# A state-space layer and a gated feed-forward in one kernel: the second x tile and the second up row change queues, and the first tile runs ahead alone

## The chip, the core and the metric

The kernel runs on one core of a Trainium2 chip. A core has a matrix engine (TensorE, in the profile PE, its weight loads PEld), VectorE (DVE), ScalarE (ACT), GpSimd (POOL) and SyncE (SP). SP, ACT and POOL issue transfers (DMAs); ACT's and SP's go through hardware queues, POOL's through a software queue. The metric is the device time of one execution in microseconds (us), and the shown time is the median over several executions.

## The reference

For x of 2048 tokens and 512 features, with xn the layer norm of x:

```python
xn = _layernorm(x, axis=-1)
return x + _A_ref(xn, ...) + _B_ref(xn, w_gate, w_up, w_down)

# _A_ref: a diagonal complex state-space model of 512 states
Bu = jnp.einsum("bld,pd->blp", x + 0j, B_bar)
h = Lam_bar[None, :] * h + Bu[:, t, :]          # for each t of 2048
y = 2.0 * jnp.einsum("blp,dp->bld", hseq, Cmat).real + x * Dskip

# _B_ref: a gated feed-forward with 1376 hidden features
return (silu(x @ w_gate) * (x @ w_up)) @ w_down
```

Inputs, weights and output are bfloat16. The products run in bfloat16 with sums in float32.

## The kernel before, in words

The 2048 tokens are cut into 16 tiles of 128, and these into four chunks of 512. For each chunk the kernel does the projection into the states (`bproj_tile`, L382), the scan over time (VectorE, L429, with rotations around it), the gate and up products (`gu_mm`, L459), and the two products that give the output (`out_ffn` L623, `out_ssm` L633). The 1376 hidden features are ten blocks of 128 and a last part of 96, which has a function of its own (`gateup_last`, L548): sixteen small matmuls into two PSUM banks, two activations and two copies on ACT, and a product on VectorE that is put into the list `products` and issued later, together with the transpose of the result.

TensorE's order is written out by hand. VectorE's work for scans, tables and norms stands in a backlog with costs, and `pump(us)` issues as much of it as the given matmul time covers; `multiply(keep)` issues waiting products until `keep` are left. Every engine works off its own instructions in the order in which the code issues them.

Chunk 0 starts differently from the others, since nothing is loaded yet. Its first three tiles have the tokens as the fixed operand of the matmul and the weights as the moving one, so that the work can follow the weights row by row: a "row" (`load_row`, L121) is 128 of the 512 input features of a weight for hidden features 0 to 1023, 128 x 1024 values or 256 KB. There are four up rows (`wu01`, indices 0 to 3), four gate rows (`wg01`), and one transfer each for the remaining features (`w_end`). All of these are issued by SP in one line, behind tile 0 of x; tile 1 of x is issued by ACT. A VectorE memset of two elements of tile 1 stands ahead of that ACT transfer, which therefore waits for it. POOL loads three small parameter vectors.

For tiles 0 and 1 the normalization does not wait for the statistics. `sum_dve` (L228) sums each token's features on VectorE; `raw_mm` (L240) transposes the raw tile on TensorE, in four blocks `k` of 128 features; `cT_mean` (L244) subtracts the mean in the same PSUM bank with a further matmul; `raw_copy` (L248) copies each block to SBUF (`xcT`), the even ones on ACT, the odd ones on VectorE. These blocks are the fixed operands of `row_mm(which, k)` (L747, matmuls at L506), which multiplies row `k` with both tiles and both halves of the features: four matmuls of 512 columns. The factor 1/std is applied when ACT takes the result out of PSUM (`sw_up` L522, `sw_gate` L512).

The order at the head is: sums of both tiles, transposes of tile 0, half of its means and copies, transposes of tile 1, the other means, the other copies, then `row_mm` for up rows 0 to 3, the statistics (`ln_stats` L188) of tiles 0 and 1, gate rows, and tiles 2 and 3. Then follow the rest of chunk 0's features (L813), the projection of chunk 0 (L865), which needs the transposed weight `BT` (`load_bt`, L148), `gateup_last(0)` (L878), and chunk 1's projection.

Of the kernel before, what the change touches and what calls it, by code (L numbers as in the profile page):

```python
# [23 lines left out]
def kernel(  # L24
# [17 lines left out]
    nc = tc.nc  # L42
# [9 lines left out]
    KD = D // 128  # L52
# [25 lines left out]
    def bank(shape=(128, CW), dtype=F32):  # L78
        return psum.tile(list(shape), dtype, name="ps")

    def flat(ap3):
        return ap3.rearrange("p q j -> p (q j)")

    x_v = A_x[0].rearrange("(n p) d -> p n d", p=128)
    out_v = out[0].rearrange("(n p) d -> p n d", p=128)
    wg_v = B_w_gate.rearrange("(k p) f -> p k f", p=128)
    wu_v = B_w_up.rearrange("(k p) f -> p k f", p=128)


    xall = const.tile([128, NT, D], BF16, name="xall")  # L90
# [5 lines left out]
    wu01 = const.tile([128, KD, FE], BF16, name="wu01")  # L96
# [24 lines left out]
    def load_row(q, t, view, k):  # L121
        q.dma_start(out=t[:, k, :], in_=view[:, k, 0:FE])  # L122

    HK = KD // 2
# [1 line left out]
    make_identity(nc, ident[:])  # L126
    minus_mean = const.tile([128, 128], BF16, name="minus_mean")
    nc.sync.dma_start(out=xall[:, 0, :], in_=x_v[:, 0, :])  # L128
    nc.vector.memset(xall[:, 1, 0:2], 0.0)
    nc.scalar.dma_start(out=xall[:, 1, :], in_=x_v[:, 1, :])  # L130
    nc.scalar.preload_act_table_set("silu_and_others")
    for k in range(KD):
        load_row(nc.sync, wu01, wu_v, k)
    for k in range(HK):
        load_row(nc.sync, wg01, wg_v, k)
# [49 lines left out]
    def by_k(ap):  # L185
        return ap.rearrange("p (k d) -> p k d", d=128)
# [36 lines left out]
    sums = const.tile([128, 2], BF16, name="sums")  # L223
# [4 lines left out]
    def sum_dve(i, dst):  # L228
        nc.vector.scalar_tensor_tensor(out=xnT[:, NCH - 1, i, 0:HW], in0=xall[:, i, 0:HW], scalar=1.0,
                                       in1=xall[:, i, HW:D], op0=ALU.mult, op1=ALU.add, accum_out=dst)  # L230
# [3 lines left out]
    raw = [pair[0][1] + pair[1][0], pair[1][1] * 2]  # L234

    def cT_mm(ps, src, k, first, stop):
        nc.tensor.matmul(ps[:, k * 128:(k + 1) * 128], lhsT=src[:, k * 128:(k + 1) * 128], rhs=ident[:], start=first,  # L237
                         stop=stop)

    def raw_mm(i):  # L240
        for k in range(KD):
            cT_mm(raw[i][k], xall[:, i, :], k, all(p is not raw[i][k] for p in raw[i][:k]), False)

    def cT_mean(i, *ks):  # L244
        nc.tensor.matmul(by_k(raw[i][ks[0]][:])[:, ks[0]:ks[-1] + 1:HK], lhsT=sums[:, i:i + 1].to_broadcast([128, 128]),
                         rhs=minus_mean[:, None, :].to_broadcast([128, len(ks), 128]), start=False, stop=True)

    def raw_copy(i, k):  # L248
        cT_copy(V.tensor_copy if k % 2 else nc.scalar.copy, raw[i][k], i, k, k + 1)

    def cT_copy(copy, ps, i, k0=0, k1=KD):
        copy(out=xcT[:, k0:k1, i * 128:(i + 1) * 128], in_=by_k(ps[:, k0 * 128:k1 * 128]))
# [21 lines left out]
    V = nc.vector  # L274
# [107 lines left out]
    def bproj_tile(c, part, q):  # L382
        if c not in u_tiles:
            u_tiles[c] = ssm.tile([128, 2, NQ, CW], BF16, name="u16", bufs=2)
        ps = bank()
        for k in range(KD):
            nc.tensor.matmul(ps[:] if c else by_k(ps[:]), lhsT=BT[:, part, k, q * 128:(q + 1) * 128],  # L387
                             rhs=xnT[:, c, k, :] if c else xnT0[:, k], start=(k == 0), stop=(k == KD - 1))
        nc.scalar.copy(out=u_tiles[c][:, part, q, :], in_=ps[:])  # L389
# [67 lines left out]
    products = []  # L457
# [10 lines left out]
    def gu_tile(c):  # L468
        if c not in gu_tiles:
            gu_tiles[c] = gut.tile([128, FT, CW], BF16, name="guT")  # L470
        return gu_tiles[c]
# [8 lines left out]
    def gu_rest(c):  # L480
        return gu_more_rest[:] if c == 2 else gu_tile(c)[:, FT - 1, 0:RT * 128]
# [21 lines left out]
    def sw_mm(ps, groups, gi, i, k0=0, k1=KD):  # L503
        a, b = fgroups[gi]
        for k in range(k0, k1):
            nc.tensor.matmul(ps[:, 0:(b - a) * 128], lhsT=tokens(i, k), rhs=groups[gi][:, k, 0:(b - a) * 128],  # L506
                             start=(k == 0), stop=(k == KD - 1))
# [35 lines left out]
    def g0_dma(a, b):  # L543
        nc.sync.dma_start_transpose(out=runs(gu_tiles[0][:, a:b, :]), in_=g0[:, a:b].rearrange("p f i d -> p (f i d)"))
# [3 lines left out]
    def gateup_last(c):  # L548
        gl = g_last[c % 2][:] if c else g0[:, FT - 1, 0:RT]
        u = up_p.tile([128, RT, 128], BF16, name="ul", bufs=2)  # L550
        for h in range(0, TPC, 2):
            ps = bank()[:, 0:4 * FR].rearrange("p (i w f) -> p i w f", i=2, w=2)
            for i in range(2):
                for k in range(KD):
                    nc.tensor.matmul(ps[:, i],  # L555
                                     lhsT=xnT[:, c, k, (h + i) * 128:(h + i + 1) * 128] if c else xnT0[:, k, h + i, :],
                                     rhs=w_end[:, k, :, FL - FE:FL - FE + FR], start=(k == 0), stop=(k == KD - 1))
            two = slice(h * RB, (h + 2) * RB)
            src = ps.rearrange("p i w (j f) -> p w j i f", f=RB)
            nc.scalar.activation(out=gl[:, :, two].rearrange("p j (i f) -> p j i f", f=RB), in_=src[:, 0], func=ACT.Silu)  # L560
            nc.scalar.copy(out=u[:, :, two].rearrange("p j (i f) -> p j i f", f=RB), in_=src[:, 1])

        def product():
            V.tensor_tensor(out=gl, in0=gl, in1=u[:], op=ALU.mult)
            if c:
                nc.sync.dma_start_transpose(out=gu_rest(c).rearrange("p (n t) -> p n t", t=128),
                                            in_=gl.rearrange("p i d -> p (i d)"))
            else:
                a = fgroups[1][1]
                n = (FT - 1 - a) * TPC + RT  # L570
                nc.sync.dma_start_transpose(
                    out=flat(gu_tile(0)[:, a:FT, :])[:, 0:n * 128].rearrange("p (n t) -> p n t", t=128),
                    in_=g0[:, a:FT].rearrange("p f i d -> p (f i d)")[:, 0:n * 128])
        products.append(product)
# [93 lines left out]
    def step():  # L668
        for item in backlog[0:AHEAD + 1]:
            if item[2] is not None:  # L670
                item[2]()
                item[2] = None
        cost, op, _, _ = backlog.pop(0)
        op()
        owed[0] -= cost

    def pump(us):

        owed[0] += us
        while backlog and owed[0] >= backlog[0][0] * 0.5:  # L680
            step()
        if not backlog:
            owed[0] = 0.0

    def multiply(keep):

        while len(products) > keep:
            products.pop(0)()
            owed[0] -= 0.65

    def need(tag):

        while any(item[3] == tag for item in backlog):
            step()


    GU = 8 * 0.2163
# [29 lines left out]
    dummy(warm, 4, CW)  # L727
    dummy(warm, 5, 128)
    nc.vector.tensor_scalar(out=minus_mean[:], in0=ident[:], scalar1=-1.0 / D, scalar2=None, op0=ALU.mult)
    for i in range(2):  # L730
        sum_dve(i, sums[:, i:i + 1])
    raw_mm(0)
    for k in range(HK):
        cT_mean(0, k)
        raw_copy(0, k)
    raw_mm(1)
    for k in range(HK, KD):
        cT_mean(0, k)
    for k in range(HK):
        cT_mean(1, k, k + HK)  # L740
        raw_copy(1, k)
    for k in range(HK, KD):
        raw_copy(0, k)
    for k in range(HK, KD):
        raw_copy(1, k)

    def row_mm(which, k):  # L747
        for i in range(2):
            for gi in range(2):
                sw_mm(pair[which][i][gi], (U, G)[which], gi, i, k, k + 1)  # L750

    for k in range(KD):
        row_mm(0, k)
    for i in range(2):
        ln_stats(i)
        ln_rstd(i, i + 1)
# [3 lines left out]
    for n in range(2):  # L760
        norm_dve(n)
    row_mm(1, 0)
    pp = prm_transpose()
    ln_stats(2)
# [6 lines left out]
    for k in range(1, SW):  # L771
        row_mm(1, k)
# [48 lines left out]
    def bproj_chunk(c):  # L821
        need(f"ln{c}")
        for part in range(2):
            for q in range(NQ):
                bproj_tile(c, part, q)
                pump(BP)
                multiply(0 if q else 1)
# [34 lines left out]
        queue(f"ssm{c}", fwd + back)  # L862

    need("ln0")
    for part in range(2):  # L865
        for q in range(NQ):
            bproj_tile(0, part, q)
            pump(BP)
            multiply(0 if q else 1)
# [5 lines left out]
    queue("cf", c_ops())  # L875
    need("ln1")
    g0_dma(0, fgroups[1][1])
    gateup_last(0)  # L878
    pump(GU / 2)
    bproj_chunk(1)  # L880
    load_down()
    for part, src in enumerate((A_C_re, A_C_im)):
# [62 lines left out]
```

## Time and profile before

| what | us |
|---|---|
| median of 3 runs | 177.39 (177.05 to 178.04) |
| the profiled execution's own time | 178.12 |
| its span, first to last instruction | 176.0 |
| TensorE busy | 171.0 |
| VectorE busy | 157.4 |
| ScalarE busy | 102.3 |
| GpSimd busy | 27.1 |

How to read it: times in the views are microseconds from the span's start. A row of the timeline has start, duration, engine, line, operation, output and input tiles, shapes and a count; behind it in brackets the idle time of that engine just ahead and what ended it. In a list of waits, a row has the waiting engine and line, what it waited for, the total, the number of times and the longest. In the table by stretches, a row has the stretch, its length, busy time and number of instructions of PE, PEld, DVE, ACT and POOL, the clock granted to TensorE, the busy share of the DMA engines and GB/s. The chain that ended last gives start, duration and place of each piece. Matmuls overlap, so that several of them in a row take less than the sum of their durations.

### The profile page before, as it was taken

How to read it: one execution, taken by the hardware profiler on the slowest of the kernel's cores; microseconds unless marked ns; L12 is line 12 of the kernel's file. 1: busy time of each engine (PE TensorE's matmuls, PEld its weight loads, DVE VectorE, ACT ScalarE, POOL GpSimd, SP SyncE). 2: the span in 40 equal slices, each digit the busy share in tenths (PEclk: the TensorE clock that was granted, in tenths of full speed). 3: DMA queues.
4: the chain of work that ended last, by engine and by line, in shares of the span. 5: the costliest groups of instructions: out<-in, count | busy, mean ns of one | idle time of the engine just before them, and what ended most of it. 6: DMA issues, size and time to landing. Idle time of an engine off the chain costs nothing.

```text
span 176.0 us, 2435 instructions
## 1 busy us (share of the span) xinstructions
PE 171.0 (97%) x878; PEld 82.0 (47%) x894; DVE 157.4 (89%) x260; ACT 102.3 (58%) x188; POOL 27.1 (15%) x36
## 2 busy tenths in 40 slices
PE   8899999999999999999999999999999999999993
PEld 5444445564444464444444444446444444444542
DVE  3767999999999999999999999999999999589642
ACT  3179589794996689976044362014666652983100
POOL 5234110022000000000302500014100000530700
PEclk9999999999999999999999999999999999999999
DMA  5998969999999300220005830006310000597741
GB/s 152 370 342 80 194 110 181 303 202 293 169 207 274 115 4 0 50 61 0 2 4 111 94 34 0 0 4 68 53 22 0 0 4 0 70 164 124 93 89 60
DMA packets 34027, 18.05 MB, mean 103 GB/s; under 512 B 24512, under 2 KB 32832, under 8 KB 33888
## 3 DMA queue, kind: packets, MB, share of 16 engines
q1 hardware_dynamic: 30272, 14.39, 35.0%
q0 software_dynamic: 3456, 3.28, 14.6%
q10 hardware_dynamic: 288, 0.23, 0.4%
q8 instruction: 7, 0.11, 0.3%
q14 instruction: 4, 0.03, 0.1%
HBM read 8.33 MB, written 5.24 MB: 77 GB/s over the span
## 4 chain that ended last, share of the span: by engine, by line
PE 94%; DMA 3%; issue 1%; SPq 0%; ACT 0%; DVE 0%; ACTq 0%
PE ps L462 29%; PE ps L630 20%; PE ps L643 16%; PE ps L387 16%; PE ps L506 7%; PE ps L555 3%; DMA wu<-in_B_w_up_dram 3%; PE ps L805 2%; PE ps L620 2%; ACT u L489 0%; SPq L122 0%; SPq L128 0%; DVE xall L646 0%; PE ps L237 0%; PE ps L278 0%
## 5 line engine op out<-in xcount | busy, mean ns | idle before, releaser
L429 DVE TENSOR_TENSOR_SCAN g<-r_t,car,u 128x512 bf16<-128x512 f32 x24 | 28.8, 1263 | 0.0
L643 PE MATMUL ps<-CF,wt 128*128 128x512 bf16 (+2 forms) x133 | 28.2, 366 | 0.2
L387 PE MATMUL ps<-xnT,BT 128*128 128x512 bf16 x125 | 28.1, 379 | 0.2
L630 PE MATMUL ps<-wd_sb,guT 128*128 128x512 bf16 (+2 forms) x129 | 26.5, 362 | 0.1
L462 PE MATMUL ps<-xnT,wu 128*128 128x512 bf16 x94 | 24.5, 379 | 0.2
L462 PE MATMUL ps<-xnT,wg 128*128 128x512 bf16 x93 | 24.3, 379 | 0.1
L389 ACT CAST u<-ps 128x512 bf16<-128x512 f32 x32 | 17.8, 591 | 5.0 <-PE ps L387 4.1
L489 ACT CAST u<-ps 128x512 bf16<-128x512 f32 x30 | 17.8, 592 | 4.8 <-PE ps L462 4.8
L643 PEld LDWEIGHTS <-wt 128*128 128x128 bf16 x136 | 12.9, 98 | 15.0 <-DVE xall L600 0.4
L387 PEld LDWEIGHTS <-BT 128*128 128x128 bf16 x128 | 12.5, 98 | 14.9 <-DMA BT<-in_A_B_re_dram 0.3
L630 PEld LDWEIGHTS <-guT 128*128 128x128 bf16 x130 | 12.4, 98 | 13.8
L199 POOL TENSOR_TENSOR rstd<-ve,neg_half 128x1 f32<-128x1 f32 (+1 forms) x7 | 7.0, 1001 | 73.0 <-DVE ve L198 72.6
L652 ACT CAST res<-ps 128x512 bf16<-128x512 f32 x12 | 6.9, 582 | 18.5 <-PE ps L643 18.5
L592 ACT ACTIVATE xr<-xall,nb,rstd 128x512 bf16<-128x512 bf16 x16 | 11.8, 804 | 8.7 <-DVE xall L600 5.0
L653 POOL DMA_DIRECT2D out_dram<-res x12 | 10.5, 1043 | 35.6 <-ACT res L652 30.0
L462 PEld LDWEIGHTS <-wu 128*128 128x128 bf16 x96 | 9.4, 98 | 11.3
L488 ACT ACTIVATE guT<-ps 128x512 bf16<-128x512 f32 x20 | 12.1, 604 | 4.0 <-PE ps L462 3.6
L462 PEld LDWEIGHTS <-wg 128*128 128x128 bf16 x96 | 9.3, 98 | 10.6
L212 ACT ACTIVATE xn<-xall,nb,rstd 128x512 bf16<-128x512 bf16 x8 | 6.3, 816 | 8.8 <-DVE nb L202 8.8
L189 DVE BATCH_NORM_STATS2 stats<-xall 128x6 f32<-128x512 bf16 x16 | 10.8, 675 | 0.6 <-DMA xall<-in_A_x_dram 0.6
L462 PE MATMUL ps<-xnT,w_end 128*128 128x512 bf16 x47 | 10.8, 379 | 0.1
L397 DVE TENSOR_TENSOR pm<-g,c 128x2048 bf16<-128x2048 bf16 x8 | 9.8, 1222 | 0.1
(132 smaller groups left out, 235.3 us busy)
## 6 DMA issues: line engine op xcount, KB each, us to landing
out_dram<-in_A_x_dram SPq DMA_DIRECT2D x8, 192.0 KB, 3.2
out_dram<-res POOLq DMA_DIRECT2D x12, 128.0 KB, 3.1
out_dram<-xall POOLq DMA_DIRECT2D x3, 512.0 KB, 6.4
wd_sb<-in_B_w_down_dram SPq DMA_DIRECT2D x1, 1280.0 KB, 7.8
wu<-in_B_w_up_dram SPq DMA_DIRECT2D x4, 256.0 KB, 4.9
wg<-in_B_w_gate_dram SPq DMA_DIRECT2D x4, 256.0 KB, 5.5
xall<-in_A_x_dram SPq DMA_DIRECT2D x1, 1024.0 KB, 7.0
xall<-in_A_x_dram SPq DMA_DIRECT2D x1, 512.0 KB, 6.1
```

What stands on the lines that cost most here:

```text
L189: nc.vector.bn_stats(out=stats[:, n, 0, :], in_=xall[:, n, :])
L387: nc.tensor.matmul(ps[:] if c else by_k(ps[:]), lhsT=BT[:, part, k, q * 128:(q + 1) * 128], rhs=xnT[:, c, k, :] if c else xnT0[:, k], star ...
L389: nc.scalar.copy(out=u_tiles[c][:, part, q, :], in_=ps[:])
L429: V.tensor_tensor_scan(out=g()[:, part, q, :], data0=r_t[:, q:q + 1].to_broadcast([128, CW]), data1=u_tiles[c][:, part, q, :], initial=ini ...
L462: nc.tensor.matmul(ps[:fs, lo:hi], lhsT=wslice(groups, fi, k), rhs=xnT[:, c, k, lo:hi], start=(k == 0), stop=(k == KD - 1))
L488: nc.scalar.activation(out=gu(c, fi, fi + 1)[:fs, 0, :], in_=psg[:fs], func=ACT.Silu)
L489: nc.scalar.copy(out=u_pair[c][:fs, fi % 2, :], in_=psu[:fs])
L506: nc.tensor.matmul(ps[:, 0:(b - a) * 128], lhsT=tokens(i, k), rhs=groups[gi][:, k, 0:(b - a) * 128], start=(k == 0), stop=(k == KD - 1))
L592: nc.scalar.activation(out=box["xr"][:], in_=xall[:, n, :], func=ACT.Identity, scale=rstd[:, n:n + 1], bias=nb[:, n:n + 1])
L630: nc.tensor.matmul(o_tiles[n, b][:, 0:hi - lo], lhsT=gu(c, fi, fi + 1)[:, 0, i * 128:(i + 1) * 128], rhs=wd_sb[:, fi, lo:hi], start=(fi == ...
L643: nc.tensor.matmul(o[:, 0:hi - lo], lhsT=w_tiles[c][:, part, q, i * 128:(i + 1) * 128], rhs=CF[:, part, q, lo:hi], start=False, stop=(part ...
L653: nc.gpsimd.dma_start(out=out_v[:, n, lo:hi], in_=res[:, lo:hi], accum_op=ALU.add)
```

## The change

Up row 1 is issued by ACT where tile 1 of x was, with the small memset now in that row; SP issues tile 1 of x behind up row 0, and then up rows 2 and 3. VectorE sums tile 0 alone at first. TensorE prepares tile 0 completely, then multiplies it with up rows 0 and 1; only then is tile 1 summed, transposed and copied, with all four copies on ACT. Row 2 follows for tile 0, rows 0 to 2 for tile 1, and row 3 for both. Last, the matmuls of `gateup_last(0)` stand ahead of chunk 0's projection, and its product is taken out of the list and put back at its old place, so that VectorE's order stays as it was.

```diff
-    nc.vector.memset(xall[:, 1, 0:2], 0.0)
-    nc.scalar.dma_start(out=xall[:, 1, :], in_=x_v[:, 1, :])
+    nc.vector.memset(wu01[:, 1, 0:2], 0.0)
+    load_row(nc.scalar, wu01, wu_v, 1)
     nc.scalar.preload_act_table_set("silu_and_others")
-    for k in range(KD):
+    load_row(nc.sync, wu01, wu_v, 0)
+    nc.sync.dma_start(out=xall[:, 1, :], in_=x_v[:, 1, :])
+    for k in range(HK, KD):
         load_row(nc.sync, wu01, wu_v, k)
...
-        cT_copy(V.tensor_copy if k % 2 else nc.scalar.copy, raw[i][k], i, k, k + 1)
+        cT_copy(V.tensor_copy if k % 2 and i == 0 else nc.scalar.copy, raw[i][k], i, k, k + 1)
...
-    for i in range(2):
-        sum_dve(i, sums[:, i:i + 1])
+    def row_mm(which, k, tiles=range(2)):
+        for i in tiles:
+            for gi in range(2):
+                sw_mm(pair[which][i][gi], (U, G)[which], gi, i, k, k + 1)
+
+    sum_dve(0, sums[:, 0:1])
     raw_mm(0)
-    for k in range(HK):
+    for k in range(KD):
         cT_mean(0, k)
         raw_copy(0, k)
+    for k in range(HK):
+        row_mm(0, k, (0,))
+    sum_dve(1, sums[:, 1:2])
     raw_mm(1)
-    for k in range(HK, KD):
-        cT_mean(0, k)
     for k in range(HK):
         cT_mean(1, k, k + HK)
+    for k in range(KD):
         raw_copy(1, k)
-    for k in range(HK, KD):
-        raw_copy(0, k)
-    for k in range(HK, KD):
-        raw_copy(1, k)
...
-    for k in range(KD):
-        row_mm(0, k)
+    row_mm(0, HK, (0,))
+    for k in range(HK + 1):
+        row_mm(0, k, (1,))
+    row_mm(0, KD - 1)
...
     need("ln0")
+    gateup_last(0)
+    pump(GU / 2)
+    last0 = products.pop()
     for part in range(2):
...
     g0_dma(0, fgroups[1][1])
-    gateup_last(0)
-    pump(GU / 2)
+    products.append(last0)
     bproj_chunk(1)
```

Here `KD` is 4 and `HK` is 2.

More of the change, by code (lines that the diff above doesn't have):

```diff
@@ L729 @@
     nc.vector.tensor_scalar(out=minus_mean[:], in0=ident[:], scalar1=-1.0 / D, scalar2=None, op0=ALU.mult)
-    for i in range(2):
-        sum_dve(i, sums[:, i:i + 1])
+    def row_mm(which, k, tiles=range(2)):
[3 more added lines that the diff above has]
+    sum_dve(0, sums[:, 0:1])
     raw_mm(0)
-    for k in range(HK):
+    for k in range(KD):
         cT_mean(0, k)
         raw_copy(0, k)
+    for k in range(HK):
+        row_mm(0, k, (0,))
+    sum_dve(1, sums[:, 1:2])
     raw_mm(1)
-    for k in range(HK, KD):
-        cT_mean(0, k)
     for k in range(HK):
         cT_mean(1, k, k + HK)
+    for k in range(KD):
         raw_copy(1, k)
-    for k in range(HK, KD):
-        raw_copy(0, k)
-    for k in range(HK, KD):
-        raw_copy(1, k)
[L747 to L750, printed above, removed]
-    for k in range(KD):
-        row_mm(0, k)
+    row_mm(0, HK, (0,))
+    for k in range(HK + 1):
+        row_mm(0, k, (1,))
+    row_mm(0, KD - 1)
     for i in range(2):
```

## The prediction

> **What bounds the kernel now.** I read the engines' totals first, then the waits of TensorE, then the chain that ended last, and then the first ten microseconds in order of time.
>
> ```profile
> span 176.0 us, 2435 instructions
> PE 171.0 (97%) x878; PEld 82.0 (47%) x894; DVE 157.4 (89%) x260; ACT 102.3 (58%) x188; POOL 27.1 (15%) x36
> ```
> ```profile
> PE ps L703 <- PEq L929: 0.8, 1, 0.8
> PE ps L506 <- DMA wu<-in_B_w_up_dram: 0.6, 1, 0.6
> ```
>
> TensorE is busy for 97% of the span, and its list of waits has only two entries: the program's start, and one wait of 0.6 us for an up row. The chain tells the same story.
>
> ```profile
> 1.20 0.41 SPq L122
> 1.61 0.04 issue
> 1.65 4.80 DMA wu<-in_B_w_up_dram
> 6.45 0.04 issue
> 6.49 3.61 PE ps L506 x16
> ...
> 22.47 0.86 PE ps L805 x4
> 23.33 6.91 PE ps L387 x32
> 30.24 1.32 PE ps L555 x16
> ```
>
> It runs from the second of the four up rows (row 1, issued at 1.65, landed at 6.45) into TensorE and never leaves it for more than a moment. So the end of the kernel is the time at which TensorE gets through the up rows, plus work without gaps. Whatever the change does to the moment when the first gate matmul starts (9.08 below) comes out at the end unreduced; everything later has to be shown to stay hidden.
>
> The head in order of time (tile 0 and tile 1 are the first two 128-token tiles of x):
>
> ```profile
> 0.90 0.37 ACTq L130 DMA_DIRECT2D xall<-in_A_x_dram  x1
> 3.07 0.42 DVE L229 SCALAR_TENSOR_TENSOR xnT<-xall 128x256 bf16<-128x256 bf16 x1 [1.53 <-DMA xall<-in_A_x_dram]
> 3.09 0.61 PE L237 MATMUL ps<-ident,xall 128*128 128x128 bf16 x4
> 3.48 0.43 DVE L229 SCALAR_TENSOR_TENSOR xnT<-xall 128x256 bf16<-128x256 bf16 x1
> 3.56 0.39 PE L245 MATMUL ps<-minus_mean,sums 128*128 128x128 bf16 x2
> 3.75 0.63 PE L237 MATMUL ps<-ident,xall 128*128 128x128 bf16 x4
> 3.89 0.27 ACT L252 CAST CF<-ps 128x128 bf16<-128x128 f32 x1 [1.30 <-PE ps L245]
> 4.18 0.85 PE L245 MATMUL ps<-minus_mean,sums 128*128 128x128 bf16 x4
> 4.82 1.07 PE L506 MATMUL ps<-wu,CF 128*128 128x512 bf16 x4
> 4.85 0.60 ACT L252 CAST CF<-ps 128x128 bf16<-128x128 f32 x3 [0.69 <-PE ps L245]
> 5.67 0.68 DVE L189 BATCH_NORM_STATS2 stats<-xall 128x6 f32<-128x512 bf16 x1
> 6.49 2.75 PE L506 MATMUL ps<-wu,CF 128*128 128x512 bf16 x12 [0.60 <-DMA wu<-in_B_w_up_dram]
> 9.08 1.03 PE L506 MATMUL ps<-wg,CF 128*128 128x512 bf16 x4
> 9.55 0.69 DVE L189 BATCH_NORM_STATS2 stats<-xall 128x6 f32<-128x512 bf16 x1 [0.60 <-DMA xall<-in_A_x_dram]
> ```
>
> Four matmuls of row 0 are done by 5.89, TensorE stands until 6.49, and twelve more take it to 9.08: (9.08 - 6.49) / 12 = 0.216 us each. Now the transfers, as busy time of each engine and, last, the DMA engines' share and GB/s:
>
> ```profile
> 2.00:2.50 0.50, 0.50 (x3) 0.20 (x2) 0.00 (x0) 0.50 (x1) 0.50 (x2) 1.00 0.93 285
> 2.50:3.00 0.50, 0.50 (x6) 0.41 (x4) 0.00 (x0) 0.09 (x1) 0.50 (x1) 1.00 1.12 367
> 3.00:3.50 0.50, 0.50 (x6) 0.34 (x4) 0.43 (x3) 0.00 (x0) 0.50 (x2) 1.00 1.11 389
> 3.50:4.00 0.50, 0.50 (x7) 0.44 (x6) 0.42 (x4) 0.11 (x1) 0.04 (x1) 1.00 0.80 111
> 4.00:4.50 0.50, 0.50 (x7) 0.50 (x6) 0.29 (x1) 0.15 (x1) 0.00 (x0) 1.00 1.04 226
> 4.50:5.00 0.50, 0.50 (x4) 0.34 (x3) 0.00 (x0) 0.15 (x1) 0.00 (x0) 1.00 0.95 320
> ```
> ```profile
> L506 PE MATMUL ps<-wu,CF x16: 376/379/427, 4.8 to 8.9; 128*128 128x512 bf16 x16
> DMA to landing us min/median/max: 2.9/4.9/5.2
> ```
>
> Two things are to be seen. The DMA engines are full from about 2.5 us on (shares of 0.93 to 1.12), except for a dip between 3.5 and 4.5 where they are occupied but move little. And row 0 (the 2.9 in the second fence, issued at 1.20) lands at 4.1, just before that dip, while row 1 takes 4.8 us. Summing GB/s times 0.5 us gives 697 kB by 4.5 and 857 kB by 5.0. Tile 0, tile 1, row 0 and row 1 are 128 + 128 + 256 + 256 = 768 KB, or 786 kB, which on average had moved by about 4.8. Row 1 yet landed at 6.45: some of the engines lag behind the mean by more than a microsecond, and a landing needs all of them.
>
> **The change, part by part.**
>
> *Order of transfers.* Row 1 takes tile 1's place on the Activation queue (same place, one issue of 0.37 us), tile 1 goes behind row 0 on SP. SP has five issues ahead of the gate rows in both kernels, so rows 2 and 3 and all that follows are issued at the same places, and the bytes ahead of each are the same. The later transfers that wait on an early one's slot (gate row 2 and x 3 now behind up rows 1 and 0, gate row 3 behind tile 1) have a backlog in front of them; I cost this at nothing, with delays under a microsecond hidden by that backlog.
>
> What lands when? Before, row 1 was the last of 768 KB; now tile 1 is the last of the same 768 KB. With full DMA engines, tile 1 inherits row 1's landing, 6.45. Row 0 shares the engines with row 1 and comes later than 4.1; row 1 comes earlier. Bounds for tile 1's landing T: 4.8 (the mean engine) and 6.45 (the slowest). I take the upper for the sum, because it is the measured landing of the same amount of data, and keep the lower for the range.
>
> In sentences of their own: the Trainium skill, "DMA: Bandwidth & Descriptors", section "Issuing engines are not separate DMA queues", says that transfers from all issuing engines end on the same 16 DMA engines and interleave, and that a second issuing engine saves only issue time. By that rule T stays at 6.45; if the Activation queue were a road of its own, SP's 512 KB up to tile 1 would land as early as row 0 did, at 4.1. The full shares with both queues active (1.12 from 2.5 to 3.0) agree with the rule.
>
> *Order of TensorE.* Before, four matmuls stand before the wait and twelve behind: first gate matmul at T + 0.04 + 12 x 0.216 = T + 2.63 (or 5.89 + 2.59 = 8.48 where T is under 5.85). After, tile 1's preparation stands behind the wait instead. From T: the DVE sum and the step to the mean matmul (3.07 to 3.56) with the 0.04 of the wake-up, 0.53; mean to the copy's start (3.56 to 3.89), 0.33; the copy, 0.27; wake-up, 0.04. That is T + 1.17. The transposes of tile 1 lie beside the sum, the two tile-0 matmuls of row 2 (0.43) lie beside mean and copy. Then ten matmuls are left (rows 0 to 2 of tile 1, row 3 of both): 2.16. The first gate matmul starts at T + 3.33. The four copies are now all on ACT, at 0.20 each (0.60 for three) against 0.43 us of matmuls per row, so they do not hold it up; VectorE saves two copies.
>
> The difference is 3.33 - 2.63 = +0.70 us at T = 6.45. The gap has not gone; a transfer with a longer tail behind it now ends it. At T = 5.5, before would start the gate rows at 8.48 and after at 8.83, +0.35; the two are equal at T = 5.15.
>
> *Queued behind the new wait on VectorE.* Tile 1's sum now stands ahead of the statistics of tile 0, which move from 5.67 to T + 0.55 = 7.0, 1.33 later. VectorE's idle 0.60 before 9.55 takes part of that; the rest, 0.73, goes on to tile 2.
>
> ```profile
> 10.50 0.35 DVE L226 TENSOR_SCALAR CF<-xall,mv 128x512 bf16<-128x512 bf16 x1
> 11.51 0.43 PEld L237 LDWEIGHTS <-CF 128*128 128x128 bf16 x4
> 23.10 6.65 PEld L387 LDWEIGHTS <-BT 128*128 128x128 bf16 x32 [0.26 <-DMA BT<-in_A_B_re_dram]
> 38.15 2.35 DVE L397 TENSOR_TENSOR pm<-u,s 128x2048 bf16<-128x2048 bf16 x2
> ```
>
> Tile 2's centring would end at 10.85 + 0.73 = 11.58, and its transposes come at 11.51 + 0.70 = 12.21: hidden. The rest of VectorE's work is 0.73 later with a TensorE that is 0.70 later.
>
> *Last features of chunk 0 first.* Sixteen matmuls (1.32 us in the chain) move from behind the projection to ahead of it. The number is the same, so this costs nothing by itself. It could gain only a wait for BT; the weight load waited 0.26 us for it, but TensorE itself goes from 22.47 + 0.86 to 23.33 without a gap. Gain nothing; were TensorE 0.5 us earlier or BT 0.7 later, these 1.32 us would cover it. The projection's outputs come 1.32 us later on ACT; their first reader on VectorE starts at 38.15, some 7 us behind the projection's end at 30.24. The product is held back to its old place.
>
> The sum: the profiled execution took 178.12 us (176.0 and 2.1 around it), so 178.8 with the same landings. That execution is 0.73 above the median of 177.39; part of that may be its own 0.6 us wait. Against the median the sum gives 178.1 at T = 6.45 and 177.75 at T = 5.5. I take 178.0, nearer the measured landing.
>
> **The rivals.**
>
> *Tile 1 lands early; faster.* The dip between 3.5 and 4.5 may catch other packets now, with two queues open. If tile 1 landed at 4.8, TensorE would be bound by its own work: tile 0's first copy ends at 4.16, so matmuls from about 4.3, sixteen of them (3.46) and tile 1's preparation (0.43 from 3.75 to 4.18), 8.2 in all. That is 0.88 under 9.08 and 0.28 under 8.48: 176.5 to 177.1. It decides from T under 5.15. For it: the mean engine is there at 4.8. Against it: a landing needs the slowest. Chance 0.15.
>
> *The change does not do what it says.* The landings move about as much as the tail behind them costs (T near 5.2): 177.4. Chance 0.20.
>
> *A slow array.* The weight loads of the 512-column warm-up matmuls show their pace:
>
> ```profile
> 1.16 0.15 PEld L703 LDWEIGHTS <-const-bfloat16-1.0 128*128 128x128 bf16 x1 [0.28 <-issue]
> 1.59 0.15 PEld L703 LDWEIGHTS <-const-bfloat16-1.0 128*128 128x128 bf16 x1 [0.28 <-issue]
> ```
>
> One in 0.43 us, half the rate of the 0.216 later. TensorE now has nothing from about 4.3 until row 0 lands, which by the shared engines may be at 5.7. If that idle kept the array slow for eight more matmuls, 8 x 0.21 = 1.7 us would be added: 179.8. Against it: the 0.6 us without work before did not slow the twelve matmuls behind it. Chance 0.10. The Trainium skill, "TensorE: Matmul & The Clock Gate", section "What's actually happening", says that the clock goes to full rate after a busy window of some 3.4 us and that the windows run freely; by it a thinner first window could postpone full rate by one window.
>
> **How the numbers follow.** My forecast, tile 1 ending the wait late and the kernel 0.3 to 1.0 us slower, has 0.55, with its own range 177.7 to 178.6. The measurement can tell about 0.5%, 0.89 us, from no change: 176.5 to 178.28. The forecast lies mostly inside; its upper end (before's median without a gap, 8.48, against 6.45 + 3.33 = 9.78, which is +1.3) lies outside, and with the slow array gives 0.24 for slower. The early landing must be set against a before with its gap to pass 0.5%: 0.06. Within 0.5%: 0.70. The range reaches from 176.9, inside the early case, to 178.8, the sum on the profiled execution.
>
> **What would show it.** Right: a wait of VectorE's L231 and TensorE's L247 for tile 1, ended by an x transfer landing near 6 us; the first gate matmul near 9.4 to 9.8; the 16 matmuls of the last features directly behind L805's last ones, and no new wait beyond 10 us. Wrong: tile 1 landing by 5, the first gate matmul at 8.5 or before, or TensorE waiting for row 0 and then running at 0.43 us a matmul.

## The result and the profile after

The changed kernel takes 178.39 us (median of 22 executions, 177.86 to 180.01) against 177.64 us (177.05 to 178.43): +0.75 us, ratio 1.0046 with a 95% interval of 1.0033 to 1.0059. That is slower, clear of no change; the interval lies on both sides of the 0.5% that the prediction took as the limit of what can be told from no change. The totals and TensorE's list of waits, from the profile of the changed kernel:

```profile
span 176.4 us, 2434 instructions
PE 171.7 (97%) x878; PEld 82.0 (46%) x894; DVE 157.1 (89%) x258; ACT 103.6 (59%) x190; POOL 27.1 (15%) x36
```
```profile
PE ps L705 <- PEq L931: 0.8, 1, 0.8
PE ps L508 <- ACT CF L254: 0.2, 1, 0.2
```

The wait for an up row, 0.6 us before, is gone from this execution, and yet the span is 0.4 longer. The head in order of time (start, duration, engine and line; the lines are two higher than before):

```profile
3.26 0.43 DVE L231 SCALAR_TENSOR_TENSOR xnT<-xall 128x256 bf16<-128x256 bf16 x1 [1.72 <-DMA xall<-in_A_x_dram]
3.28 0.61 PE L239 MATMUL ps<-ident,xall 128*128 128x128 bf16 x4
4.08 0.48 ACT L254 CAST CF<-ps 128x128 bf16<-128x128 f32 x2 [1.49 <-PE ps L247]
4.60 1.86 PE L508 MATMUL ps<-wu,CF 128*128 128x512 bf16 x4 [0.24 <-ACT CF L254]
4.91 0.42 DVE L231 SCALAR_TENSOR_TENSOR xnT<-xall 128x256 bf16<-128x256 bf16 x1 [0.22 <-DMA xall<-in_A_x_dram]
5.41 0.15 PEld L508 LDWEIGHTS <-CF 128*128 128x128 bf16 x1 [0.28 <-issue]
5.83 0.15 PEld L239 LDWEIGHTS <-xall 128*128 128x128 bf16 x1 [0.28 <-issue]
6.26 0.61 PE L239 MATMUL ps<-ident,xall 128*128 128x128 bf16 x4
6.92 2.75 PE L508 MATMUL ps<-wu,CF 128*128 128x512 bf16 x12
9.09 0.69 DVE L191 BATCH_NORM_STATS2 stats<-xall 128x6 f32<-128x512 bf16 x1 [0.54 <-DMA xall<-in_A_x_dram]
9.51 1.03 PE L508 MATMUL ps<-wg,CF 128*128 128x512 bf16 x4
```

Tile 1 is there at 4.9, far ahead of its use; its sum runs at 4.91 and its transposes only at 6.26. In between TensorE is at its four matmuls of rows 0 and 1, and its weight loads stand 0.43 us apart: the array still runs at half pace (it had changed to 0.22 before its matmuls at 4.82 in the profile of before). The granted clock in the tables by stretches reads 1.00 in every stretch of both heads, so the pace is read from this spacing. Four matmuls take from 4.60 to 6.26, then comes tile 1's preparation, and behind the last twelve, at full pace, the first gate matmul stands at 9.51 against 9.08. The transfers issued behind each other (issue at 0.90 for the row on the Activation queue, 1.66 for tile 1, 2.13 for row 2; the last column is the time from there to the landing):

```profile
wu<-in_B_w_up_dram ACTq DMA_DIRECT2D x1, 256.0 KB, 3.0
...
xall<-in_A_x_dram SPq DMA_DIRECT2D x1, 128.0 KB, 3.2
...
wu<-in_B_w_up_dram SPq DMA_DIRECT2D x1, 256.0 KB, 4.1
```
```profile
3.50:4.00 0.50, 0.50 (x7) 0.38 (x6) 0.20 (x2) 0.00 (x0) 0.04 (x1) 1.00 1.00 375
4.00:4.50 0.50, 0.36 (x4) 0.20 (x2) 0.32 (x2) 0.42 (x2) 0.00 (x0) 1.00 1.18 377
```

Row 1 lands at 3.9, tile 1 at 4.9 and row 2 at 6.2, and the dip between 3.5 and 4.5 us (111 and 226 GB/s in the profile of before) is not there: 375 and 377. That is no work of the change: the next profile of the kernel before does not have the dip either.

Behind the head nothing changed. In this profile, in that of before and in eleven of the experiments, the span less the start of the first gate matmul is the same to 0.1 us but for one of them, e12 (e8 is left out; it is told of below). The labels e1 to e12 stand for the experiments that follow:

| kernel | first gate matmul, us | span, us | difference, us |
|---|---|---|---|
| before | 9.08 | 176.0 | 166.9 |
| before, again (e1) | 8.66 | 175.6 | 166.9 |
| after | 9.51 | 176.4 | 166.9 |
| after, again (e9) | 9.01 | 175.9 | 166.9 |
| last features only (e2) | 8.78 | 175.7 | 166.9 |
| transfers only (e3) | 11.76 | 178.7 | 166.9 |
| order only (e4) | 8.77 | 175.7 | 166.9 |
| order, filled (e5) | 9.91 | 176.8 | 166.9 |
| before, no warm-up (e6) | 9.49 | 176.4 | 166.9 |
| row 1 second on ACT (e7) | 9.49 | 176.4 | 166.9 |
| after, all on SP (e10) | 9.48 | 176.4 | 166.9 |
| after, filled (e11) | 9.23 | 176.1 | 166.9 |
| parameters on SP (e12) | 8.81 | 176.3 | 167.5 |

### The profile page after: what moved, and what is told of

It reads as the page before. It is cut to its first block, busy times and chain, and to the rows that moved or that the text cites. A ratio compares the mean times of both kernels' runs of the same rounds, so it can differ in the third digit from the quotient of the medians.

```text
span 176.4 us, 2434 instructions
## 1 busy us (share of the span) xinstructions
PE 171.7 (97%) x878; PEld 82.0 (46%) x894; DVE 157.1 (89%) x258; ACT 103.6 (59%) x190; POOL 27.1 (15%) x36
## 4 chain that ended last, share of the span: by engine, by line
PE 95%; DMA 1%; ACT 1%; issue 1%; DVE 0%; ACTq 0%
PE ps L464 29%; PE ps L632 20%; PE ps L645 16%; PE ps L389 16%; PE ps L508 8%; PE ps L557 3%; PE ps L805 2%; PE ps L622 2%; DMA xall<-in_A_x_dram 1%; PE ps L239 1%; ACT u L491 0%; ACT CF L254 0%; PE ps L247 0%; DVE xall L648 0%; PE ps L280 0%
## 5 line engine op out<-in xcount | busy, mean ns | idle before, releaser
L655 POOL DMA_DIRECT2D out_dram<-res x12 | 10.5, 1043 | 35.2 <-ACT res L654 30.0
```

The source lines that it names most:

```text
L655: nc.gpsimd.dma_start(out=out_v[:, n, lo:hi], in_=res[:, lo:hi], accum_op=ALU.add)
```

## The experiments

### One part at a time

**Before again.** No edit.

> The kernel before, unchanged, against itself, for a second profile of its head and for the width of the comparison. Theory A (the landing of up row 1 at 6.45 was an accident of one execution, since tile 1, the last of the same 768 KB, landed at 4.9 in the profile of after; what decides is the moment at which TensorE's pace goes from 0.43 to 0.22 us per 512 columns, 4.9 in the profile of before and 6.7 in that of after, and it falls anywhere): row 1 lands between 4.8 and 6.5, the pace changes at another time than 4.9, ratio 1.000 within 0.002. Theory B (the landing is as before in every execution, and the order on the queues mended it): row 1 lands at 6.4 again, with TensorE idle 0.5 to 0.6 us before it.

Ratio 1.0004 (0.9992 to 1.0015). TensorE's rows at the head:

```profile
4.79 1.03 PE L506 MATMUL ps<-wu,CF 128*128 128x512 bf16 x4
6.07 2.75 PE L506 MATMUL ps<-wu,CF 128*128 128x512 bf16 x12 [0.25 <-DMA wu<-in_B_w_up_dram]
8.66 1.03 PE L506 MATMUL ps<-wg,CF 128*128 128x512 bf16 x4
```
```profile
3.50:4.00 0.50, 0.50 (x7) 0.43 (x6) 0.38 (x3) 0.11 (x1) 0.04 (x1) 1.00 0.95 283
4.00:4.50 0.50, 0.50 (x7) 0.50 (x6) 0.29 (x1) 0.16 (x1) 0.00 (x0) 1.00 1.21 297
```

Row 1 landed at 6.03 and ended the wait at 6.07 here, at 6.49 in the first profile; the twelve matmuls behind it are the same. The landing varies, but in neither of the two is it near 5. Theory A's "accident" is too strong, theory B's "in every execution" too. And the dip of the first profile is gone (283 and 297 GB/s), though nothing was changed and row 1 is late all the same. Eight profiles have the x tiles and up rows in the order and on the queues of before (before, e1, e2, e4, e5, e6, e8 and e12). In these row 1 lands at 5.3 to 6.45, and the dip is in three of them (before, e2, e12) and not in the other five.

**Only the last features ahead of the projection.**

```diff
     need("ln0")
+    gateup_last(0)
+    pump(GU / 2)
+    last0 = products.pop()
...
-    gateup_last(0)
-    pump(GU / 2)
+    products.append(last0)
```

> Before, with only the last features of chunk 0 moved ahead of its projection. Both theories: no change, ratio 0.999 to 1.001, since TensorE had no gap there. If the move itself costs (ACT or VectorE later in chunk 0), up to +0.75 us (1.004) and the other parts cost nothing.

Ratio 1.0003 (0.9987 to 1.0018): no cost, no gain. Its head is that of before, and its profile shows what the array's pace costs there:

```profile
4.92 4.03 PE L506 MATMUL ps<-wu,CF 128*128 128x512 bf16 x16
8.78 1.03 PE L506 MATMUL ps<-wg,CF 128*128 128x512 bf16 x4
```

Weight loads 0.42 us apart, at 5.34 and 5.76, show that the first up matmuls ran at half pace. They filled the time until row 1 had landed at 6.07, TensorE did not wait at all, and the first gate matmul, at 8.78, lies between those of the other two.

**Only the transfers exchanged.**

```diff
-    nc.scalar.dma_start(out=xall[:, 1, :], in_=x_v[:, 1, :])
+    load_row(nc.scalar, wu01, wu_v, 1)
...
+    load_row(nc.sync, wu01, wu_v, 0)
+    nc.sync.dma_start(out=xall[:, 1, :], in_=x_v[:, 1, :])
-    for k in range(KD):
+    for k in range(HK, KD):
         load_row(nc.sync, wu01, wu_v, k)
```

> Before, with only the transfers exchanged: up row 1 on the Activation queue, tile 1 behind up row 0; TensorE's order as before, with all of tile 1's preparation ahead of row 0's matmuls. The sixteen up matmuls then start some 1.2 us behind tile 1's landing T: T + 1.2 + 3.5. With T near 4.9 (theory A) the first gate matmul comes at 9.6 to 9.9 and the kernel is 0.5 to 1.0 us slower; with T = 6.4 (theory B) at 11.1 and 2 us slower.

Ratio 1.0094 (1.0060 to 1.0128), median 179.69, +1.84 us: nearly twice the upper expectation of theory A, and near theory B's 2 us, but not by theory B's landing. TensorE's rows of its profile:

```profile
5.14 0.61 PE L239 MATMUL ps<-ident,xall 128*128 128x128 bf16 x4 [0.78 <-DMA xall<-in_A_x_dram]
5.54 0.85 PE L247 MATMUL ps<-minus_mean,sums 128*128 128x128 bf16 x4
6.18 5.74 PE L508 MATMUL ps<-wu,CF 128*128 128x512 bf16 x16
11.76 1.03 PE L508 MATMUL ps<-wg,CF 128*128 128x512 bf16 x4
```
```profile
10.03 0.15 PEld L508 LDWEIGHTS <-CF 128*128 128x128 bf16 x1 [0.28 <-issue]
10.45 1.84 PEld L508 LDWEIGHTS <-CF 128*128 128x128 bf16 x9 [0.28 <-issue]
```

Tile 1 landed at 5.1, near theory A's 4.9. But behind the 0.78 us without work the array stayed at half pace until about 10.5. The nine executions fall into two groups, 178.12 to 178.61 (three) and 179.62 to 180.65 (six), their medians 1.8 us apart. The profile is of the longest of the nine; no profile shows the pace in the lower group.

**Only TensorE's order.** The hunk of the head's order and of `raw_copy`, with the transfers and the last features as before.

```diff
+    sum_dve(0, sums[:, 0:1])
     raw_mm(0)
-    for k in range(HK):
+    for k in range(KD):
         cT_mean(0, k)
         raw_copy(0, k)
+    for k in range(HK):
+        row_mm(0, k, (0,))
+    sum_dve(1, sums[:, 1:2])
     raw_mm(1)
...
+    row_mm(0, HK, (0,))
+    for k in range(HK + 1):
+        row_mm(0, k, (1,))
+    row_mm(0, KD - 1)
```

> Before, with only TensorE's order at the head (tile 0 alone with up rows 0 and 1, then tile 1's preparation, its copies all on ACT), transfers as before: tile 1 lands early at 3.4 and up row 1 last. Then tile 0's matmuls of row 1 wait for its landing T, and tile 1's preparation, 0.43 us or more, stands behind it: first gate matmul at T + 0.04 + 14 x 0.216 + 0.43 = T + 3.5. With T = 5.0 to 5.5 (theory A): 8.5 to 9.0 at full pace, up to 9.6 with a late change of pace, +0.1 to +0.6 us. With T = 6.45 (theory B): 9.95, +0.9 us.

Ratio 1.0067 (1.0037 to 1.0096). In its profile row 1 landed at 5.27 and ended the wait at 5.31, with TensorE at full pace, and the first gate matmul came at 8.77, inside theory A's range. But that profile is of the shortest of the twelve executions, 177.79; less 166.9 us, the spans of the twelve put the first gate matmul at 9.65 in the median, an estimate. Again two groups: eight executions from 177.79 to 178.80, and four from 179.89 to 180.40, with no profile of the upper one. Either part alone, transfers or order, costs no less than both together, so the loss is not a sum of the two.

### The pace of the array

**The idle stretch filled.**

```diff
-    for k in range(HK):
-        row_mm(0, k, (0,))
+    row_mm(0, 0, (0,))
+    dummy(pair[1][1][1], 8, 128)
+    row_mm(0, 1, (0,))
```

> The kernel with only TensorE's order changed, and eight matmuls of 128 columns without use between tile 0's matmuls with up row 0 and those with up row 1, where TensorE stood idle for 0.64 us. Theory A (an idle stretch before the change of pace can make the array miss it, and it then stays slow for some 3.4 us more, 1.7 us of time: the 4 of 12 executions of that kernel at 179.9 to 180.4, against 177.8 to 178.8): no execution above 179.5, the median within 0.3 us of 178.5. If the high executions have another cause, a third of them stay above 179.8, and all are up to 0.4 us slower for the added matmuls. It computes the same output.

Ratio 1.0052 (1.0032 to 1.0071); seven executions, 178.36 to 179.11. The upper group did not appear. With seven executions a third of them being absent by chance is not likely (0.67 to the seventh power is 0.06, and the third itself is known from twelve executions only), and it agrees with the idle stretch as its cause; it is not more than that.

**No warm-up matmuls.**

```diff
-    dummy(warm, 4, CW)
-    dummy(warm, 5, 128)
```

> Before, without the nine matmuls on constants that stand ahead of tile 0. Theory A (the pace of TensorE changes some 3.4 us behind the start of steady work): work begins at 3.1, the pace changes between 6.5 and 10, the first gate matmul comes at 9.1 to 10.7 against 8.7 to 9.1, 0.4 to 2 us slower, 1.1 in the median. If the transfers alone set the head (row 1 lands at 6.0 to 6.5 in any case), under 0.2 us.

Ratio 1.0030 (1.0010 to 1.0049), +0.5 us. The rows of its profile:

```profile
4.58 5.07 PE L506 MATMUL ps<-wu,CF 128*128 128x512 bf16 x16
9.49 1.03 PE L506 MATMUL ps<-wg,CF 128*128 128x512 bf16 x4
```

Row 1, landed at 6.1, is not waited for, because the four matmuls ahead of it at half pace last until then. The pace does set the first gate matmul, but its loss is at the lower end of the expectation: before hides the first four slow matmuls behind row 1's transfer.

### The transfers

**Row 1 as a second transfer on the Activation queue.**

```diff
     nc.scalar.dma_start(out=xall[:, 1, :], in_=x_v[:, 1, :])
+    load_row(nc.scalar, wu01, wu_v, 1)
...
-    for k in range(KD):
+    for k in (0, 2, 3):
         load_row(nc.sync, wu01, wu_v, k)
```

> Before, with up row 1 as a second transfer on the Activation queue behind tile 1 of x; TensorE's order as before. If the two queues together bring the first 768 KB in by 4.9 to 5.1, as in the profiles of after and of the kernel with only the transfers exchanged, row 1 is no longer waited for and the first gate matmul comes at 8.3 plus half of what the change of pace is later than 4.8, 0.1 to 0.4 us faster in the median. If the last of 768 KB lands at 6.0 to 6.5 in whatever order and queue, no change within 0.1%.

Ratio 1.0009 (0.9994 to 1.0024): no gain. Row 1 lands earlier, at 5.6, but row 0, which shares the engines with it, at 5.4 and not at 4.1, and TensorE waits for row 0 from 4.9 to 5.47. The wait has only changed its row. (This profile is of the longest of its twelve executions, 178.45, with the first up matmuls at half pace; the median is 177.93.)

**The parameters on the Activation queue.**

```diff
-        nc.gpsimd.dma_start(out=prm_rows[i * NQ:(i + 1) * NQ, :], in_=v.rearrange("(q j) -> q j", j=128))
+        nc.scalar.dma_start(out=prm_rows[i * NQ:(i + 1) * NQ, :], in_=v.rearrange("(q j) -> q j", j=128))
     nc.scalar.preload_act_table_set("silu_and_others")
```

> Before, with the three small parameter vectors issued on the Activation queue behind tile 1 of x, and not by GpSimd through the software queue. If the software queue's transfers make the dip between 3.5 and 4.5 us (111 and 226 GB/s), the dip goes, row 1 lands by 4.9 and the kernel is 0.1 to 0.4 us faster. If they do not, row 1 lands at 6.0 to 6.5 as before: no change, or up to 0.2 us slower for the later table load on ACT.

Ratio 1.0494 (1.0469 to 1.0518), a miss by the edit's own fault: the three issues came only at 6.44, 8.17 and 8.88, ACT stood behind them until 9.16, which the profile puts down to the landing of a gate row, and ACT's copies behind that kept TensorE waiting. The transfers ahead of all this had no dip (287 and 287 GB/s) and row 1 landed at 5.46, but e1 had no dip either, with the software queue in use, so this says nothing on that queue.

```profile
PE ps L506 <- ACT CF L252: 5.9, 1, 5.9
```

**The parameters on SP, behind the second gate row.** The same lines with `nc.sync`, placed there.

> Before, with the three small parameter vectors issued by SP behind the second gate row, and not by GpSimd through the software queue. In the kernel that issued them late on the Activation queue, row 1 landed at 5.46 and 3.5 to 4.5 us moved 287 GB/s, against 6.0 to 6.5 and 111 to 226 in before. If the software queue causes the dip: row 1 lands at 5.0 to 5.5, TensorE does not wait for it, and the median falls by 0.1 to 0.3 us (0.9985 to 0.9995). If x tiles 2 and 3, which are now issued later, come too late for VectorE, it rises by up to 0.5 us.

Ratio 1.0057 (1.0033 to 1.0080), slower by more than either branch had it. Its expectation took the dip for a property of before, which e1 contradicts. In its profile the dip is there without any software transfer, and row 1 lands at 6.2:

```profile
3.50:4.00 0.50, 0.50 (x7) 0.50 (x7) 0.39 (x3) 0.21 (x1) 0.00 (x0) 1.00 1.06 168
4.00:4.50 0.50, 0.50 (x8) 0.48 (x7) 0.19 (x1) 0.05 (x1) 0.00 (x0) 1.00 0.69 143
```

So the dip does not need the software queue; what makes it come in some executions is open. The first gate matmul starts at 8.81, no later than in before; the extra 0.6 us of this kernel lies behind TensorE's end (its last VectorE operation starts at 173.04, before's at 173.31, and its span is still longer), and its cause was not settled.

### The changed kernel again, and two variants of it

> The changed kernel, unchanged, for a second profile of its head beside the next two. Whatever the cause, the ratio is 1.003 to 1.006 again, and the span is 166.9 us longer than the start of the first gate matmul, as in all profiles so far. Theory C (three things delay it: tile 0 lands 0.3 later beside a 256 KB row, TensorE runs the first matmuls at the slow pace, and the wait for row 1 is followed by one for row 2, which lands at 6.2 with 2.6 us of matmuls behind it): tile 0 lands at 3.2 to 3.5, tile 1 by 5.1, the first gate matmul comes no earlier than 8.8. Theory B (tile 1's landing with 3.3 us behind it): tile 1 near 6 and the gate rows 3.3 later.

Ratio 1.0065 (1.0039 to 1.0092), a little above the range expected. Tile 0 landed at 3.3, tile 1 at 4.9, and this time the pace was full from the first up matmul:

```profile
4.62 1.02 PE L508 MATMUL ps<-wu,CF 128*128 128x512 bf16 x4 [0.41 <-DMA wu<-in_B_w_up_dram]
5.48 0.39 PE L239 MATMUL ps<-ident,xall 128*128 128x128 bf16 x4
5.71 0.38 PE L247 MATMUL ps<-minus_mean,sums 128*128 128x256 bf16 x2
6.42 2.75 PE L508 MATMUL ps<-wu,CF 128*128 128x512 bf16 x12 [0.33 <-DMA wu<-in_B_w_up_dram]
```
```profile
wu<-in_B_w_up_dram SPq DMA_DIRECT2D x1, 256.0 KB, 4.3
```

This is the clearest view of the change, in one of the shorter executions of its twelve (178.11, median 178.47). TensorE waits 0.41 us for row 0, which now lands at 4.6, and 0.33 us for row 2 (issued at 2.13, landed at 6.4), and behind that second wait stand twelve matmuls, as many as stood behind row 1 before. 6.42 + 2.59 = 9.01. Of its twelve executions, three lie at 179.59 to 179.68, the others at 177.60 to 178.77.

**All early transfers on SP.**

```diff
-    load_row(nc.scalar, wu01, wu_v, 1)
...
     load_row(nc.sync, wu01, wu_v, 0)
+    load_row(nc.sync, wu01, wu_v, 1)
     nc.sync.dma_start(out=xall[:, 1, :], in_=x_v[:, 1, :])
```

> The changed kernel with all early transfers on SP, in the order tile 0, up rows 0 and 1, tile 1, up rows 2 and 3; nothing on the Activation queue (the memset of two elements, which only held that transfer back, is left out). Theory C: tile 0 lands at 2.8 or before, TensorE starts up to 0.4 us earlier, and of the 0.75 us some 0.2 to 0.4 go: ratio to before 1.002 to 1.004. If tile 0's company on the other queue does not matter: as the changed kernel, 1.004 to 1.005, or slower where tile 1 lands near 6 as the last of 768 KB on one queue.

Ratio 1.0043 (1.0026 to 1.0061), not told apart from the changed kernel. Tile 0 landed at 2.8, so TensorE's first up matmuls came at 4.07 and not at 4.6, but tile 1 landed at 5.8 (3.7 behind its issue at 2.12) and row 2 at 6.9 (4.3 behind 2.60):

```profile
4.07 1.55 PE L507 MATMUL ps<-wu,CF 128*128 128x512 bf16 x4
5.85 0.40 PE L238 MATMUL ps<-ident,xall 128*128 128x128 bf16 x4 [0.23 <-DMA xall<-in_A_x_dram]
6.32 0.39 PE L246 MATMUL ps<-minus_mean,sums 128*128 128x256 bf16 x2
6.90 2.75 PE L507 MATMUL ps<-wu,CF 128*128 128x512 bf16 x12 [0.18 <-ACT CF L253]
9.48 1.03 PE L507 MATMUL ps<-wg,CF 128*128 128x512 bf16 x4
```

What tile 0 gains, the later landings take back; the first up matmuls run at half pace here too, 1.55 us for four. The twelve matmuls again start when row 2 has landed. The row names ACT's copies of tile 1, but the first two of the twelve are tile 0's with row 2 and need none of these; row 2 landed at 6.86, and 0.04 us behind a landing is also where the waits for rows ended in before and in e9.

**The changed kernel with its idle stretches filled.**

```diff
-    dummy(warm, 5, 128)
+    dummy(warm, 7, 128)
...
+    dummy(pair[1][1][1], 3, 128)
     for k in range(HK):
         row_mm(0, k, (0,))
```

> The changed kernel with five more matmuls of 128 columns without use, two behind the warm-up ones and three between tile 0's means and its first up matmuls, where TensorE stood idle for 0.1 and 0.24 us. If those idle stretches put off the change of pace in a share of the executions, the median falls by 0.1 to 0.4 us and no execution is over 179.2. If not, they cost what they last beyond the idle time, up to 0.15 us. The output is the same.

Ratio 1.0038 (1.0023 to 1.0052), twelve executions from 177.82 to 178.55, median 178.27 against 178.47 of the changed kernel beside it. No execution lies in the upper group (the changed kernel had 3 of 12 there in the same session, and 2 of 22 above 179.3 in the first), and the rest is where it was. That agrees with the filled stretches as what takes out the rare long delay, but none in twelve can also be chance. Filling does not bring the kernel back to before: in its profile the first up matmuls are still at half pace, with weight loads at 5.00 and 5.42, row 2 has landed at 6.4, ahead of the twelve matmuls at 6.64, and the first gate matmul comes at 9.23. No version here beats before.

## Why the prediction was right, and where it was not

**The size.** +0.70 us was worked out, and +0.75 measured; 178.0 was forecast, and 178.39 measured: inside the range, and within 0.5%, as given the largest chance. That the sum fits so well is luck. With tile 1's measured landing of 4.9, its own term gives 4.9 + 3.33 = 8.2 for the first gate matmul, earlier than before; measured were 9.51 and 9.01, for reasons that the sum does not hold. Of the signs named in advance, one of each kind came: the gate matmul at 9.51 as for right, tile 1 landing by 5 as for wrong.

**What bounds the kernel: right.** A delay of the first gate matmul reaches the end unreduced; the difference of 166.9 us in twelve of thirteen profiles shows it more sharply than the chain could.

**The step that failed is tile 1's landing T.** It was said that tile 1, as the last of the same 768 KB, inherits row 1's 6.45. It landed at 4.9 to 5.1 in the four profiles with row 1 first on the Activation queue and tile 1 on SP (after, e3, e9, e11), where row 1 as the last of 768 KB landed at 5.3 to 6.45 in eight (6.45 in before, 6.0 in e1, 5.3 in e4). On SP alone (e10) tile 1 landed at 5.8. The rule that the Trainium skill gives on "DMA: Bandwidth & Descriptors", section "Issuing engines are not separate DMA queues", holds in that the bytes take the same engines: row 0 and tile 0 came later when row 1 went beside them (row 0 at 4.6 to 4.8 and not at 3.9 to 4.4, tile 0 at 3.2 to 3.5 and not at 2.8 to 3.1). To conclude from it that the last landing stays was too much: with the same 768 KB, and the same order, it differed by more than a microsecond from execution to execution (5.3 to 6.45), and with row 1 first on the second queue it was below all of these. Why is open; the dip is not the reason, since row 1 landed at 6.0 in e1 without it.

**The tail behind the wait: half right.** That a wait with a longer tail ends the head was right, but it is another wait. The prediction had no term for the landings of rows 2 and 3. In e9 and e10, row 2's landing at 6.4 and 6.9 starts the last twelve matmuls, as row 1's did before. The term from tile 1's landing to its mean matmul, 0.53, measured 6.32 - 5.81 = 0.51 in e10, the one run where it mattered; but there too row 2, at 6.9, was the later. In after and e11 row 2 had landed, at 6.2 and 6.4, before its turn came; there TensorE's own work at half pace set the time.

**The slow array: a rival with a chance of 0.10 that turned out to be part of the loss.** In the first profile of after, TensorE waits for no transfer and loses at half pace, 1.66 us for four matmuls that take 0.86 at full pace. In the order before, those matmuls lie in the shadow of row 1's transfer (e2: half pace at first, and the first gate matmul at 8.78; e6: with no warm-up at all only +0.5 us). And an idle stretch went with a much later change of pace in the one profile taken of a long execution, e3's. Groups of executions stand above the others there and in e4 and e9, their medians 1.4 to 1.8 us apart, near the 1.7 us estimated for this rival, and two single ones in after; there are none in e5 and e11, where the stretch was filled, and none of the 108 executions of before is above 178.65. That the upper groups of e4, after and e9 have e3's cause is argued and not shown. The Trainium skill, "TensorE: Matmul & The Clock Gate", section "What's actually happening", states free-running windows of about 3.4 us, of which one must be busy; the traces agree as far as e3's 0.78 us idle went with slow pace until 10.5, while e1, with no such stretch ahead of its up matmuls at 4.79, ran these at full pace.

**The last features: right**, 1.0003. **VectorE's delay of 0.73: did not arise**, since tile 1 came early; tile 0's statistics started at 5.26, earlier than the 5.67 before.

**Tile 1 landing early: the rival came true in its condition, not in its gain.** Tile 1 did land near 4.9, under the 5.15 at which it was to decide. Its 8.2 us for the first gate matmul left out row 0's later landing, 4.6, and row 2, and took TensorE to be at full pace throughout.

How the 0.75 us divides between row 2's landing, the slow pace and the rare long delay is not settled: the two profiles of before and the two of after differ by 0.39 us on average (9.26 against 8.87), as the times of these four executions do (0.41), so the rest of the 0.75 lies in which executions were profiled. That it arises at the head can be estimated: less 166.9 us, the spans put the first gate matmul at 9.4 and 9.55 in the median for after (22 and 12 executions), and at 8.7 to 8.9 for before (three sets of 24 to 32).

## What to carry to other kernels

When a wait for one transfer of a full queue is removed, look at what the next transfer in the line has behind it: here, in e9 and e10, row 1's wait became row 2's, with the same twelve matmuls to follow. Work that stood in a gap ahead of a transfer was free here; the same work between two pieces of the bound engine's work was paid for, in after, e10 and e11 at the array's slow pace. Where nearly every profile has the same length behind one instruction, that instruction's start is a finer measure than the whole time. And one profile is one execution: see first where its time lies among the others, and do not take a feature for the kernel's before a second profile shows it, as the dip did not.

## What the runs showed that was not expected

The last landing of the same 768 KB was at 4.9 to 6.45 us; it was earliest, 4.9 to 5.1, in the four profiles with up row 1 first on the Activation queue and tile 1 behind up row 0 on SP. The dip in the transfers between 3.5 and 4.5 us comes and goes from execution to execution, and does not need the software queue: it was 168 and 143 GB/s with none of its transfers under way. An idle stretch of TensorE of 0.8 us, ahead of the change from 0.43 to 0.22 us per 512 columns, went with half pace until 10.5 us in e3; kernels with idle stretches at the head had groups of executions 1.4 to 1.8 us slower, and a few small matmuls without use put there (eight in e5; two and three more in e11) went with their absence.
